# A fused attention and feed-forward kernel: the first VectorE pass over a converted piece of weights is asked for five steps behind GpSimd's clamp in place of two

## The chip, the cores and the metric

The kernel runs on one core of a Trainium2 chip. The metric is the device time of one execution in microseconds (us). Three runs of the kernel before took 936.31, 938.56 and 933.61 us; their median, 936.31 us, is the time before. A further execution was profiled, and all durations below come from it.

The engines are called by their short names: PE (TensorE, the matmuls), DVE (VectorE), ACT (ScalarE), POOL (GpSimd) and SP (SyncE, which here only issues DMAs).

## The reference

The reference is a local and global attention whose output goes through a two-layer feed-forward network with an ELU in between. The weights arrive as float64, and the kernel turns them into pairs of float16 numbers.

```python
# attention: batch 8, heads 8, 512 local and 32 global rows, head_dim 64
s_g = scale * (q_g @ concat(k_g, k_l)^T);  out_g = softmax(s_g) @ concat(v_g, v_l)
s_l = scale * (q_l @ concat(k_g, k_l)^T), local part masked to |i - j| <= 32
out_l = softmax(s_l) @ concat(v_g, v_l)
# feed-forward: x is the attention's output, 4352 rows of 512
h = x @ w_in                       # w_in 512 x 2048, w_out 2048 x 512
g = where(h > 0, h, exp(min(h, 0)) - 1)
return g @ w_out
```

## The kernel before, in words

Two streams of work are written by one loop at the end of `attn_ffn`. The attention goes through its slots in steps, each a stage of scores, softmax, transposes or values. The feed-forward stream (FFN) takes blocks of 256 rows of x: a first product with w_in (L319), the ELU (L329 to L341), and a second product with w_out. The loop tells how many steps of the FFN have to be done by a given step of the attention. In the first 66 steps of the attention, the lead, the FFN does nothing, since no weights are there yet.

The weights come in 16 units of 128 x 1024 numbers: eight pieces (p = 0 to 7) of w_in (m = 0) and eight of w_out (m = 1) in turn. Each goes through these steps (`unit`, from L172):

- `fetch`, L169: SP asks for the raw piece (1 MB) into `raw`, of which there are two buffers. The piece two units later can't be asked for until the last step that reads this one has run.
- s0: ACT takes the absolute value of the upper halves into `cu` (L183), and POOL clamps it (L184). `cu` has three buffers.
- s1a: DVE shifts the clamped number to its place (L188). This is the pinned pass: `keep_in_program_order` holds it at its place in the order in which the code asks for things.
- s1b and s1c: DVE puts in the upper bits (L191) and the lower bits (L195) of the raw piece.
- s1d: ACT takes the absolute value with the largest per partition (L199). It is the last reader of the raw piece.
- s2 and s3, "the spread": the largest over all partitions through a transpose on PE (L136) and a reduction on DVE (L137), then a power of two and its inverse on DVE (L126, L127, L131), and the high float16 part on ACT (L208).
- s4: the low float16 part on DVE (L211).

Steps are put off with `defer(n, fn)`, which runs fn n ticks later; a tick is a step of the attention in the lead, and a step of the FFN stream (about six matmuls) behind it. What a tick sets is when an instruction is asked for. The order in which each engine then runs its instructions is made from that by the tile framework's scheduler when the program is built, which may move an instruction on its engine; only those under `keep_in_program_order` (L188 and the transpose of L136) stay where they were asked for. On the chip each engine runs its instructions strictly in the order so made, and waits at each for what it needs.

The pieces fall into groups: a (piece 0), b (piece 1), c (2 and 3), d (4 to 7). As soon as a group is converted, `tables` makes its scales: the product of the powers on DVE (L227, L228), the largest over the partitions, and the table that `choose` waits for before it gives out a job of that group. The first four blocks of x are computed group by group, and their sums go out to DRAM (`od`) and come back (L451 adds them) for the next group. Once all pieces are converted there is the table "f", and all other blocks are computed in one go with seven products in place of eight (L478).

A job needs x split in float16 parts as well: its largest (L571, and L136/L137 again), a power of two (L126 to L131), the high part on ACT (L565), the low part on DVE (L568), and its scales on POOL (L581 to L585). In the attention, L753 (DVE) and L759 (ACT) are the scores' softmax, L763 and L764 (DVE) and L766 (POOL) its norm, L797 (PE) and L799 (DVE in the lead, ACT behind it) the transposes, L803 (PE) the product with v and L836 (ACT) its copy into x.

Of the kernel before, what the change touches and what calls it, by code (L numbers as in the profile page):

```python
# [60 lines left out]
def attn_ffn(ctx: ExitStack, tc: tile.TileContext, qT, qgT, kT, vT, w_in, w_out, mask, out):  # L61
# [23 lines left out]
    def defer(n, fn):  # L85
        if n == 0:
            return fn()
        later.setdefault(now[0] + n, []).append(fn)
# [10 lines left out]
    lead = [True]  # L99
# [23 lines left out]
    def power(dst, src):  # L123

        dst = dst.bitcast(I32)
        nc.vector.tensor_scalar(dst, src.bitcast(I32), 0x7f800000, None, ALU.bitwise_and)  # L126
        nc.vector.tensor_scalar_max(dst, dst, LOW)  # L127

    def inverse(dst, src):

        nc.vector.tensor_scalar(dst.bitcast(I32), src.bitcast(I32), TOP, -1.0, ALU.subtract, ALU.mult)  # L131

    def all_max(dst, src):

        tp = ps_a.tile([P, 512], F32, name="pa")
        tc.keep_in_program_order(nc.tensor.transpose(tp[:, 0:P], src.to_broadcast([P, P]), ident))  # L136
        nc.vector.tensor_reduce(out=dst, in_=tp[:, 0:P], op=ALU.max, axis=AX.X)  # L137
# [15 lines left out]
    def load_weights():  # L153
        todo = [(group, m, p) for group in "abcd" for p in range(*GROUPS[group]) for m in range(2)]
        raws = [fetch(*todo[0][1:])]
        yield
        for n, (group, m, p) in enumerate(todo):
            if n + 1 < len(todo):
                raws.append(fetch(*todo[n + 1][1:]))
            unit(m, p, raws[n])  # L160
            if (m, p) == (1, GROUPS[group][1] - 1):
                defer(12, lambda group=group: tables(group))
                if p == NP - 1:
                    defer(13, lambda: tables("f"))
            yield

    def fetch(m, p):
        raw = ffn.tile([P, NC, 2 * P, 2] if m == 0 else [P, 2, DM, 2], I32, name="raw")
        nc.sync.dma_start(raw, w1[:, :, 2 * p * P:2 * (p + 1) * P, :] if m == 0 else w2[:, 2 * p:2 * p + 2, :, :])  # L169
        return raw  # L170

    def unit(m, p, raw):  # L172
        f = slice(2 * p * P, 2 * (p + 1) * P)
        shape = [P, NC, 2 * P] if m == 0 else [P, 2, DM]
        parts = [w[:, :, f] for w in win] if m == 0 else [w[:, 2 * p:2 * p + 2, :] for w in wout]
        pw = (pww if m == 0 else pwo)[:, p:p + 1]
        u = ffn.tile(shape, F32, name="cu", bufs=3)
        mx = ffn.tile([P, 4], F32, name="cm", bufs=4)
        high, low = raw[..., 1], raw[..., 0]
        ui = u.bitcast(I32)  # L180

        def s0():
            nc.scalar.activation(u, high.bitcast(F32), AF.Abs)  # L183
            nc.gpsimd.tensor_scalar(u, u, FMAX, FMIN, ALU.min, ALU.max)  # L184

        def s1a():
            tc.keep_in_program_order(
                nc.vector.tensor_scalar(ui, ui, 3, 0x3ffffff8, ALU.logical_shift_left, ALU.bitwise_and))  # L188

        def s1b():  # L190
            nc.vector.scalar_tensor_tensor(out=ui, in0=high, scalar=-0x40000000, in1=ui,  # L191
                                           op0=ALU.bitwise_and, op1=ALU.bitwise_or)

        def s1c():
            nc.vector.scalar_tensor_tensor(out=ui, in0=low, scalar=29, in1=ui,  # L195
                                           op0=ALU.logical_shift_right, op1=ALU.bitwise_or)

        def s1d():
            nc.scalar.activation(low.bitcast(F32), u, AF.Abs, accum_out=mx[:, m:m + 1])  # L199

        def s2():
            if m == 0:
                all_max(mx[:, 1:2], mx[:, 0:1])

        def s3():
            power(pw, mx[:, 1:2])
            inverse(mx[:, 3:4], pw)
            nc.scalar.activation(parts[0], u, AF.Copy, scale=mx[:, 3:4])  # L208

        def s4():  # L210
            nc.vector.scalar_tensor_tensor(out=parts[1].rearrange("p a b -> p (a b)") if m else parts[1],  # L211
                                           in0=u.rearrange("p a b -> p (a b)") if m else u, scalar=mx[:, 3:4],
                                           in1=parts[0].rearrange("p a b -> p (a b)") if m else parts[0],
                                           op0=ALU.mult, op1=ALU.subtract)

        d = 1 if lead[0] else 2
        lag = 7 if m else 16
        for i, fn in ((1, s0), (1 + d, s1a), (1 + 2 * d, s1b), (1 + 3 * d, s1c), (1 + 4 * d, s1d),
                      (1 + lag, s2), (2 + lag, s3), (3 + lag, s4)):
            defer(i, fn)  # L220

    def tables(group):

        r = slice(*GROUPS[group])
        wm = wts.tile([P, 4], F32, name=f"wm_{group}")
        t = wts.tile([P, NP], F32, name=f"t_{group}")
        nc.vector.tensor_mul(t[:, r], pww[:, r], pwo[:, r])  # L227
        nc.vector.tensor_reduce(out=wm[:, 0:1], in_=t[:, r], op=ALU.max, axis=AX.X)  # L228

        def rest():  # L230
            all_max(wm[:, 1:2], wm[:, 0:1])
            nc.vector.reciprocal(wm[:, 2:3], wm[:, 1:2])
            nc.vector.tensor_scalar(t[:, r], pwo[:, r], wm[:, 2:3], 8.0, ALU.mult, ALU.mult)
            nc.vector.tensor_scalar_mul(isc[:, r], pww[:, r], -2.0 ** -28)
            tab[group] = wm[:, 1:2], t

        defer(5, rest)
# [736 lines left out]

    f = ffn_stream()
    units = load_weights()
    done = credit = 0

# [102 lines left out]
```

## Time and profile before

| what | value |
|---|---|
| median of three runs | 936.31 us (933.61 to 938.56) |
| profiled execution | 934.68 us |
| its span (first to last instruction) | 932.9 us |
| mean granted PE clock | 0.979 of full speed |
| the 16 conversion units | the last L188 at 176.4 us |

Three parts follow each other in the span. In the lead, to about 75 us, only the attention and the conversion of the first pieces run. Then the group jobs of the first blocks, the rest of the conversion and the attention run beside each other, to about 230 us. Behind that comes the long stretch of blocks with seven products, in which nothing is converted.

In rows of the timeline the columns are the start in us, the time in us, the engine, the line, the operation, output and input with their tiles, and how many instructions run together; in brackets stands how long the engine was idle before, and what ended the wait. In tables by stretch each engine has its busy time and its number of instructions, then come the granted PE clock, the mean share of the DMA engines and the GB/s.

### The profile page before, as it was taken

The numbers are of one execution on the slowest core, as the hardware profiler recorded it, in microseconds if no ns is written. First come the engines' busy times: TensorE is split into PE (matmuls) and PEld (weight loads), VectorE is DVE, ScalarE is ACT, GpSimd is POOL, SyncE is SP. The second block draws the span as 40 slices with busy tenths as digits, with TensorE's granted clock in tenths as the row PEclk, the third lists the DMA queues.
The fourth block names the chain that finished last, engine by engine and source line by source line (L and its number), as shares of the span: only waits on it lengthen the run. The fifth ranks groups of instructions, "written<-read, shape, count | busy, mean of one in ns | idle before, by whom it ended". The sixth has DMA issues, their size and how long they took to land.

```text
span 932.9 us, 26318 instructions
## 1 busy us (share of the span) xinstructions
PE 888.6 (95%) x10736; PEld 723.2 (78%) x10736; DVE 702.0 (75%) x1945; ACT 637.1 (68%) x1456; POOL 206.2 (22%) x413
## 2 busy tenths in 40 slices
PE   6799889799999999999999999999999999999997
PEld 3466555467676788888888888888888888888886
DVE  4869889899957768777786768786868677766566
ACT  5669888676566567675776767676766676656564
POOL 4556461441321022011122112112111121200000
PEclk7789999899999999999999999999999999999999
DMA  7957867432442134012521234103312111000000
GB/s 259 351 202 263 305 232 239 138 103 92 159 162 67 60 126 167 30 48 72 186 87 49 69 126 149 49 24 133 141 48 63 54 47 47 1 24 24 1 24 23
DMA packets 39472, 103.60 MB, mean 111 GB/s; under 512 B 5944, under 2 KB 6584, under 8 KB 39352
## 3 DMA queue, kind: packets, MB, share of 16 engines
q1 hardware_dynamic: 39064, 101.66, 31.6%
q8 instruction: 84, 1.38, 0.6%
q14 instruction: 36, 0.29, 0.1%
q10 hardware_dynamic: 288, 0.26, 0.1%
HBM read 86.70 MB, written 15.20 MB: 109 GB/s over the span
## 4 chain that ended last, share of the span: by engine, by line
PE 50%; DVE 22%; ACT 18%; DMA 5%; issue 3%; POOL 2%; SPq 0%; DVEq 0%; ACTq 0%; POOLq 0%
PE pa L319 19%; PE acc L478 9%; PE h L478 7%; ACT p L759 5%; DVE gl L341 4%; ACT gh L357 3%; DVE gx L338 3%; PE acc L443 3%; PE pa L803 3%; PE h L319 2%; DMA raw<-w_out 2%; PE pa L797 2%; DMA od<-o 2%; ACT g L329 2%; ACT g L331 2%
## 5 line engine op out<-in xcount | busy, mean ns | idle before, releaser
L319 PEld LDWEIGHTS <-winh 128*128 128x128 f16 x2160 | 209.7, 98 | 36.3 <-issue 6.6
L319 PE MATMUL pa<-xh,winh 128*128 128x256 f16 x824 | 224.9, 273 | 0.8 <-DVE xglob L873 0.8
L319 PE MATMUL pa<-xl,winh 128*128 128x256 f16 x824 | 224.7, 273 | 0.0
L319 PE MATMUL pa<-xh,winl 128*128 128x256 f16 x824 | 224.7, 273 | 0.0
L357 ACT ACTIVATE gh<-gx,xs 128x896 f16<-128x896 f32 x103 | 107.5, 1044 | 132.8 <-DVE gx L354 132.8
L766 POOL TENSOR_SCALAR p<-p,sm 128x128 f32<-128x128 f32 x256 | 117.5, 477 | 328.8 <-DVE sm L764 297.7
L341 DVE SCALAR_TENSOR_TENSOR gl<-gx,xs,gh 128x896 f16<-128x896 f32 x103 | 122.5, 1189 | 75.4 <-ACT gh L357 75.4
L478 PEld LDWEIGHTS <-gh 128*128 128x128 f16 x1456 | 140.1, 98 | 22.6 <-issue 7.0
L319 PEld LDWEIGHTS <-winl 128*128 128x128 f16 x1080 | 106.0, 98 | 16.5 <-issue 3.7
L759 ACT ACTIVATE p<-p,m 128x128 f32<-128x128 f32 x256 | 99.3, 390 | 25.8 <-DVE m L753 25.7
L478 PE MATMUL acc<-wouth,gh 128*128 128x256 f16 x312 | 85.3, 273 | 0.0
L478 PE MATMUL acc<-wouth,gl 128*128 128x256 f16 x312 | 85.1, 273 | 0.0
L331 ACT ACTIVATE g<-g 128x512 f32<-128x512 f32 x135 | 85.0, 630 | 0.1
L478 PE MATMUL acc<-woutl,gh 128*128 128x256 f16 x312 | 85.1, 273 | 0.0
L478 PEld LDWEIGHTS <-gl 128*128 128x128 f16 x728 | 71.2, 98 | 9.3 <-DVE gl L341 1.0
L329 ACT ACTIVATE g<-pa,xs 128x512 f32<-128x512 f32 x103 | 70.2, 681 | 9.7 <-PE pa L319 9.1
L478 PE MATMUL h<-raw,gh 128*128 128x256 f16 x416 | 74.3, 273 | 0.0
L319 PE MATMUL h<-xl,winh 128*128 128x256 f16 x256 | 70.7, 277 | 3.3 <-DVE xl L568 3.3
L319 PE MATMUL h<-xh,winh 128*128 128x256 f16 x256 | 70.6, 277 | 3.2 <-ACT hs L330 2.1
L319 PE MATMUL h<-xh,winl 128*128 128x256 f16 x256 | 70.7, 277 | 0.0
L803 PEld LDWEIGHTS pa<-pt,v 128*64 128x64 f32 x1728 | 53.3, 139 | 8.0 <-issue 6.3
L338 DVE SCALAR_TENSOR_TENSOR gx<-g,p 128x512 f32<-128x512 f32 x52 | 37.7, 725 | 28.3 <-ACT g L331 26.8
(219 smaller groups left out, 1878.0 us busy)
## 6 DMA issues: line engine op xcount, KB each, us to landing
v<-vT SPq DMA_DIRECT2D x64, 512.0 KB, 4.6
k<-kT SPq DMA_DIRECT2D x32, 640.0 KB, 5.2
q<-qT SPq DMA_DIRECT2D x32, 256.0 KB, 5.9
raw<-w_in SPq DMA_DIRECT2D x8, 1024.0 KB, 5.7
raw<-w_out SPq DMA_DIRECT2D x8, 1024.0 KB, 7.0
out<-o SPq DMA_DIRECT2D x32, 256.0 KB, 2.3
od<-o SPq DMA_DIRECT2D x24, 256.0 KB, 3.3
o<-od SPq DMA_DIRECT2D x24, 256.0 KB, 2.8
```

Source lines behind the costliest of these rows:

```text
L319: nc.tensor.matmul(h[:, j, :], wt[:, c, f], xt[:, c, :], start=k == 0, stop=k == 11)
L329: nc.scalar.activation(g, hf, AF.Relu, scale=sc[:, p:p + 1])
L331: nc.scalar.activation(g, g, AF.Exp, scale=-1.0)
L338: nc.vector.scalar_tensor_tensor(out=out, in0=ins[0], scalar=-1.0, in1=ins[1], op0=ALU.add, op1=ALU.max)
L341: nc.vector.scalar_tensor_tensor(out=dst, in0=src, scalar=sg, in1=hi, op0=ALU.mult, op1=ALU.subtract)
L357: nc.scalar.activation(gh, gx, AF.Copy, scale=sg)
L443: nc.tensor.matmul(acc[t], gt[:, s], wt[:, f, :], start=p == first and j == 0 and k == 0, stop=p == last and j == 1 and k == 2)
L478: nc.tensor.matmul(cols, gt, w, start=p == 0 and k == 0, stop=last and k == len(todo) - 1, skip_group_check=True)
L759: nc.scalar.activation(ps[i], ps[i], AF.Exp, bias=m[:, i:i + 1], scale=-1.0, accum_out=s[:, 0, i:i + 1])
L766: nc.gpsimd.tensor_scalar(ps[i], ps[i], s[:, 1, i:i + 1], 1.0, ALU.mult, ALU.mult)
L797: nc.tensor.transpose(tp[:, h * P:(h + 1) * P], st["p", g, t][:, h, :], ident)
L803: nc.tensor.matmul(o[:, to:to + n], st["v", g, t][:, 4 * h + w, :], st["pt", g, t][:, h, at:at + n], start=start, stop=True, skip_group_ch ...
```

## The change

All offsets are counted in ticks from the moment at which a unit is taken up; s0, with the clamp, stands at 1 in both kernels.

| step | lead before | lead now | behind the lead before | behind it now |
|---|---|---|---|---|
| s1a (L188) | 2 | 4 | 3 | 6 |
| s1b (L191) | 3 | 5 | 5 | 8 |
| s1c (L195) | 4 | 6 | 7 | 10 |
| s1d (L199) | 5 | 7 | 9 | 12 |
| s2 of w_out's units | 8 | 9 | 8 | 12 |
| s2 of w_in's units | 17 | 17 | 17 | 21 |
| tables of a group | 12 | 12 | 12 | 16 |
| tables "f" | 13 | 17 | 13 | 17 |

```diff
             if (m, p) == (1, GROUPS[group][1] - 1):
-                defer(12, lambda group=group: tables(group))
+                defer(12 if lead[0] else 16, lambda group=group: tables(group))
                 if p == NP - 1:
-                    defer(13, lambda: tables("f"))
+                    defer(17, lambda: tables("f"))
...
-        d = 1 if lead[0] else 2
-        lag = 7 if m else 16
-        for i, fn in ((1, s0), (1 + d, s1a), (1 + 2 * d, s1b), (1 + 3 * d, s1c), (1 + 4 * d, s1d),
+        d, wait = (1, 3) if lead[0] else (2, 5)
+        lag = (11 if m else 20) if not lead[0] else (8 if m else 16)
+        for i, fn in ((1, s0), (1 + wait, s1a), (1 + wait + d, s1b), (1 + wait + 2 * d, s1c), (1 + wait + 3 * d, s1d),
                       (1 + lag, s2), (2 + lag, s3), (3 + lag, s4)):
             defer(i, fn)
```

Both programs have the same instructions, 1947 on DVE and 14340 on PE among them; only their order on the engines differs, and that only from the third unit to the end of the conversion. Three places follow.

The first is DVE in the lead, around the pinned pass of the fourth unit. L799 is a copy of transposed softmax rows, L763 and L764 belong to a norm, `cm` and `pww` to a spread. Before:

```order
L799 COPY pt<-pa 128x2x4x64
L763 TENSOR_SCALAR sm<-sm 128x4
L137 TENSOR_REDUCE cm<-pa 128x1
L764 RECIPROCAL sm<-sm 128x4
L188 TENSOR_SCALAR cu<-cu 128x1024
L126 TENSOR_SCALAR pww<-cm 128x1
```

And now:

```order
L188 TENSOR_SCALAR cu<-cu 128x1024
L763 TENSOR_SCALAR sm<-sm 128x4
L799 COPY pt<-pa 128x2x4x64
L764 RECIPROCAL sm<-sm 128x4
L137 TENSOR_REDUCE cm<-pa 128x1
L191 SCALAR_TENSOR_TENSOR cu<-raw,cu 128x1024
L126 TENSOR_SCALAR pww<-cm 128x1
```

The pinned pass now stands ahead of the copy and of the norm's two small steps, and L191 ahead of the spread's L126.

The second is PE at the same place in the lead. L803 are the products with v of one slot, L797 the four transposes of another slot's softmax rows (p_83). Before:

```order
L741 MATMUL pa<-k,q 32x128 x16
L803 MATMUL h<-pt,v 64x32 x2
L797 MATMUL pa<-ident,p_83 128x128 x4
L803 MATMUL h<-pt,v 64x64 x4
L803 MATMUL h<-pt,v 64x32 x4
L803 MATMUL h<-pt,v 64x64 x4
L803 MATMUL h<-pt,v 64x32 x2
L728 MATMUL pa<-ident,pg_82 128x128 x2
```

And now:

```order
L803 MATMUL h<-pt,v 64x32 x2
L803 MATMUL h<-pt,v 64x64 x4
L803 MATMUL h<-pt,v 64x32 x4
L803 MATMUL h<-pt,v 64x64 x4
L803 MATMUL h<-pt,v 64x32 x2
L797 MATMUL pa<-ident,p_83 128x128 x4
L728 MATMUL pa<-ident,pg_82 128x128 x2
```

The four transposes have moved from within the products with v to behind them.

The third is DVE at the end of the conversion, around the split of a block of x (`xm`, `xl`) for that block's first job; the last two units are in work. Before, from the last but one unit's L191 to the last unit's L188; L568 follows eleven rows on, behind five scores' reductions (L753):

```order
L191 SCALAR_TENSOR_TENSOR cu<-raw,cu 128x1024
L714 TENSOR_REDUCE sg<-sg 128x1
L127 TENSOR_SCALAR xm<-xm 128x1
L195 SCALAR_TENSOR_TENSOR cu<-raw,cu 128x1024
L715 TENSOR_SCALAR sg<-sg 128x1
L131 TENSOR_SCALAR xm<-xm 128x1
L753 ISA p_85,m<-pa,msk 128x128
L753 ISA m 128x1
L716 RECIPROCAL sg<-sg 128x1
L188 TENSOR_SCALAR cu<-cu 128x1024
```

And now, the last unit's L188 standing seventeen rows behind the end of this piece:

```order
L127 TENSOR_SCALAR xm<-xm 128x1
L131 TENSOR_SCALAR xm<-xm 128x1
L188 TENSOR_SCALAR cu<-cu 128x1024
L714 TENSOR_REDUCE sg<-sg 128x1
L191 SCALAR_TENSOR_TENSOR cu<-raw,cu 128x1024
L211 SCALAR_TENSOR_TENSOR woutl<-cu,cm,wouth 128x1024
L715 TENSOR_SCALAR sg<-sg 128x1
L568 SCALAR_TENSOR_TENSOR xl<-xr,xm,xh 128x1024
L716 RECIPROCAL sg<-sg 128x1
L195 SCALAR_TENSOR_TENSOR cu<-raw,cu 128x1024
```

The small steps of the split (L127, L131) now stand ahead of the last but one unit's passes, and L568 ahead of the last unit's L188 and of all scores' reductions.

## The prediction

> **What bounds the kernel now.** I read the page first, then the busy times by stretch, then the waits of the pinned pass, and last the timeline of DVE, ACT, POOL and PE at the places where the order changes. The page says that PE is the bound over the whole:
>
> ```profile
> span 932.9 us, 26318 instructions
> PE 888.6 (95%) x10736; PEld 723.2 (78%) x10736; DVE 702.0 (75%) x1945; ACT 637.1 (68%) x1456; POOL 206.2 (22%) x413
> ```
>
> So time can come only from what PE spends idle (932.9 − 888.6 = 44.3 us) or at a lower clock. The table by stretch says where that is (the columns: stretch, length, busy time of each engine, granted PE clock, DMA share, GB/s):
>
> ```profile
> 0.00:77.00 77.00, 61.37 (x936) 38.59 (x937) 54.86 (x240) 49.44 (x170) 39.90 (x80) 0.82 0.75 272
> 77.00:112.00 35.00, 32.36 (x430) 22.12 (x427) 29.96 (x91) 31.26 (x74) 17.64 (x29) 0.95 0.82 277
> 112.00:135.00 23.00, 19.17 (x182) 14.28 (x167) 19.98 (x41) 21.62 (x39) 12.88 (x18) 1.00 0.78 263
> 135.00:173.00 38.00, 33.91 (x319) 20.07 (x323) 35.43 (x72) 30.12 (x56) 9.93 (x12) 1.00 0.74 231
> 173.00:186.00 13.00, 8.16 (x70) 5.42 (x55) 9.26 (x33) 7.96 (x24) 8.07 (x18) 0.74 0.19 65
> 186.00:932.00 746.00, 733.68 (x8838) 622.69 (x8835) 552.50 (x1472) 496.69 (x1098) 117.77 (x259) 1.00 0.22 77
> ```
>
> Behind 186 us PE is busy 733.68 of 746: whatever the change wins or loses earlier is carried through to the end. Ahead of it PE is idle for 15.63 us in the lead, 2.64, 3.83 and 4.09 in the three stretches from 77 to 173, and 4.84 in the 13 us at the conversion's end. The whole effect must come from there. The waits of the pinned pass are the obvious target:
>
> ```profile
> DVE cu L188 <- POOL cu L184: 6.8, 6, 2.1
> ```
>
> Six of the 16 passes waited for their clamp, 6.8 us in sum, 2.1 the longest. That is a ceiling only for what DVE gets back; PE gets it back only where PE or ACT waited for DVE behind it.
>
> **The change part by part.** The instructions are the same, so nothing is added or removed, and each term is a move. I took the places where the order differs and put the durations of before into the order of now.
>
> *Lead, 41 to 55 us.* Here are the rows of DVE, POOL, PE and ACT:
>
> ```profile
> 41.86 0.69 DVE L799 COPY pt<-pa 128x512 f32<-128x512 f32 x1
> ...
> 42.82 0.66 DVE L188 TENSOR_SCALAR cu<-cu 128x1024 int32<-128x1024 int32 x1
> ...
> 43.67 1.22 DVE L191 SCALAR_TENSOR_TENSOR cu<-raw,cu 128x1024 int32<-128x1024 int32 x1
> ```
>
> ```profile
> 41.07 0.37 POOL L766 TENSOR_SCALAR p<-p,sm 128x128 f32<-128x128 f32 x1
> 41.52 1.04 POOL L184 TENSOR_SCALAR cu<-cu 128x1024 f32<-128x1024 f32 x1
> 43.07 5.17 POOL L766 TENSOR_SCALAR p<-p,sm 128x128 f32<-128x128 f32 x8 [0.51 <-ACT p L759]
> ```
>
> ```profile
> 46.56 0.82 PE L797 MATMUL pa<-ident,p 128*128 128x128 f32 x2 [0.90 <-POOL p L766]
> ...
> 47.32 1.71 PE L803 MATMUL h<-pt,v 128*64 128x64 f32 x28
> ```
>
> ```profile
> 49.07 0.37 ACT L836 COPY xr<-h 128x256 f32<-128x256 f32 x1 [4.66 <-PE h L803]
> ...
> 50.97 1.13 ACT L199 ACTIVATE raw<-cu 128x1024 f32<-128x1024 f32 x1
> ```
>
> Before, the products L803 began, then stood behind four transposes that wait for POOL's norms, and ran on only at 47.32; ACT waited 4.66 us for them. Now the products go first. They need the copy L799. That copy now stands behind the pinned pass, which waits for the clamp's end at 41.52 + 1.04 = 42.56: the pass ends at 43.2, L763 at 43.4, the copy at 44.1. The 32 products then take about 2 us and end near 46.1, where they ended at 49.03, and ACT's L836 comes at 46.1 in place of 49.07. Behind it ACT's L199 would come up to 3.3 us earlier (50.97 less about 47.6). Against that, the norm's L764 comes behind the copy at 44.1 to 44.3, so POOL's eight norms begin at 44.3 in place of 43.07, 1.2 us later, and the transposes behind them end as much later. The bounds are −3.3 (all of ACT's gain reaches PE) and +1.2 (only the norms' delay does). I take −1.5, between them and nearer to the gain, since 4.66 us is the longer wait and the rest of the lead has 15.63 us of PE idle time to take up delays.
>
> *Group jobs, 77 to 135 us.* No order gets simpler here; the raw pieces come later. The rows are:
>
> ```profile
> 106.79 1.14 ACT L199 ACTIVATE raw<-cu 128x1024 f32<-128x1024 f32 x1
> ...
> 119.65 1.18 ACT L183 ACTIVATE cu<-raw 128x1024 f32<-128x1024 f32 x1
> ...
> 125.66 0.67 ACT L330 ACTIVATE hs<-h,xs 128x512 f32<-128x512 f32 x1
> ```
>
> ```profile
> 108.03 0.38 SPq L169 DMA_DIRECT2D raw<-w_out  x1
> ```
>
> ```profile
> raw<-w_out SPq DMA_DIRECT2D x8, 1024.0 KB, 7.0
> ```
>
> ```profile
> 120.92 1.20 POOL L184 TENSOR_SCALAR cu<-cu 128x1024 f32<-128x1024 f32 x1 [5.79 <-ACT cu L183]
> ```
>
> ```profile
> 126.38 0.27 PE L319 MATMUL h<-xh,winh 128*128 128x256 f16 x1 [1.24 <-ACT hs L330]
> ```
>
> The eighth unit's L199 (106.79) now stands on ACT behind a block's L565 and the ninth unit's L183, so at 113.6 or later, 7 us later. SP's request for the tenth unit's piece, which waits for it, goes from 108.03 to about 115, and with 7.0 us of landing ACT's L183 goes from 119.65 to about 122, the clamp's end from 122.12 to about 124.4. On POOL the scales of a job of group c now stand behind that clamp. So the evictions L329 and L330 wait for the scales, and L330 goes from 125.66 to about 127. PE waited for it already at 126.38, for 1.24 us; six matmuls of a second product that now stand ahead fill about as much. I take +0.5. Bounds: −1, if those six matmuls fill the old wait of 1.24 and nothing is late; +3.7, if the 2.4 us of L183 and the 1.3 us of L330 both reach PE, one behind the other.
>
> *135 to 173 us.* Two of the pinned pass's waits lie here, 2.6 us of DVE, and ACT has waits of its own, for landing pieces:
>
> ```profile
> ACT cu L183 <- DMA raw<-w_out: 2.5, 3, 2.1
> ```
>
> Three waits, 2.5 us, the longest 2.1. The pass's waits go; ACT's grow, since the last reader of a piece comes three ticks later and the piece is asked for as much later. A tick is about six matmuls, and the row from 112 to 135 gives 19.17 / 182 = 0.105 us for one, so three ticks are 1.9 us, called 2 from here; where DVE's shorter waits give half of it back, a piece comes 1 us later. One is set against the other: 0, with bounds −2 (DVE's 2.6 us less what PE is not waiting for) and +2.5 (ACT's waits double).
>
> *The conversion's end, 173 to 186 us.* This is the place with the most idle PE time, and the largest term:
>
> ```profile
> 169.33 1.29 DVE L211 SCALAR_TENSOR_TENSOR woutl<-cu,cm,wouth 128x1024 f16<-128x1024 f32 x1
> ...
> 173.97 0.14 DVE L131 TENSOR_SCALAR xm<-xm 128x1 int32<-128x1 int32 x1
> ...
> 176.44 0.69 DVE L188 TENSOR_SCALAR cu<-cu 128x1024 int32<-128x1024 int32 x1 [2.05 <-POOL cu L184]
> ...
> 178.10 1.61 DVE L568 SCALAR_TENSOR_TENSOR xl<-xr,xm,xh 128x1024 f16<-128x1024 f32 x1
> ```
>
> ```profile
> 172.78 1.20 ACT L183 ACTIVATE cu<-raw 128x1024 f32<-128x1024 f32 x1 [0.18 <-DMA raw<-w_out]
> ...
> 174.12 1.13 ACT L199 ACTIVATE raw<-cu 128x1024 f32<-128x1024 f32 x1
> ...
> 175.22 1.16 ACT L565 ACTIVATE xh<-xr,xm 128x1024 f16<-128x1024 f32 x1
> ...
> 184.71 0.69 ACT L329 ACTIVATE g<-h,xs 128x512 f32<-128x512 f32 x1 [3.49 <-POOL p L766]
> ```
>
> ```profile
> 176.42 0.38 PE L319 MATMUL h<-xh,winh 128*128 128x256 f16 x2 [0.71 <-ACT xh L565]
> ...
> 179.76 0.37 PE L319 MATMUL h<-xl,winh 128*128 128x256 f16 x1 [2.96 <-DVE xl L568]
> ```
>
> ```profile
> 177.50:184.20 6.70, 4.44 (x22) 3.05 (x22) 6.70 (x24) 2.91 (x14) 2.32 (x6) 0.50 0.00 0
> ```
>
> Before: the pinned pass waited 2.05 us for its clamp, with five scores' reductions and the split's L568 queued behind it; PE waited 2.96 us for that, and then ran at a clock of 0.50 for 6.7 us. Now L568 stands ahead of the pass. Its chain is shorter too: the split's L131 no longer waits behind L191 and L195 and comes near 171.0 in place of 173.97, L565 near 173.1 in ACT's free time in place of 175.22, and L568 near 174.4 to 176.0 in place of 178.10 to 179.71. That is 3.7 us for PE's first product. What is late next is ACT: L183 waits for its piece (which landed at 172.78 by the row's wait, and lands near 173.8 with the 1 us from above), behind it come L199 and eight exponentials, and I put L329 at 181.9, where it stood at 184.71: −2.8. If all 3.7 come through and the clock holds, the gain is larger: at a clock of 0.50 matmuls take twice as long, so 4.44 us busy would be about 2.2. The far end is thus 3.7 + 2.2, with some of the 0.71 ahead: −6.5. The other end is 0, if the piece lands so late that ACT's queue stands where it stood. I take −3.0, next to the −2.8 of ACT's queue. The cover of the pinned pass, now behind all this, are the reductions of two slots; without it DVE would wait the 2.05 us again, but with nobody behind it that PE needs.
>
> Tables "f" come four ticks later and the last transpose with them. PE has matmuls of group d's jobs to do until then, as many more as it takes, so I cost that at nothing; in the 746 us behind 186 PE was idle 12.3 us, and if that cover failed it would be some 1.5 us more.
>
> The sum is −1.5 + 0.5 + 0 − 3.0 = −4.0 us: 934.68 becomes 930.7. The profiled execution lies 1.63 us below the median of the three runs; against 936.31 the sum is 932.3. A measurement of this kernel can tell about 0.5%, 4.7 us, from no change: faster begins below 931.6, slower above 941.0.
>
> Two rules of the Trainium skill bear on it. The row of 0.50 from 177.5 to 184.2 follows a PE wait of 2.96 us and a stretch of thin work. The Trainium skill, "TensorE: Matmul & The Clock Gate", section on the HAM clock gate, says that the array drops to half rate after an idle window of about 3.4 us and comes back after a busy one; by that rule a shorter wait could save the whole slow stretch, and the trace agrees in so far as the slow stretch has 0.50 and follows a wait. The other row is POOL's: eight norms took 5.17 us, 0.65 each, while DVE ran L191 and L195, against 0.37 for one ahead of them. The Trainium skill, "SBUF — State Buffer", section on who interferes with whom, says that a VectorE instruction with two inputs in SBUF and a GpSimd instruction that reads SBUF shut each other out for a whole instruction. It speaks against the change in the lead: norms that begin 1.2 us later meet the same two passes, so by it that term would be +1.2, and the sum −1.3.
>
> **The rivals.** *The clock too.* If PE's first product comes 3.7 us earlier and the wait of 2.96 us shrinks, the half clock from 177.5 may not be granted at all, and the last term is −6.5 in place of −3.0; with the lead's −1.5 and nothing for the others that is −8.0, 928.3. For it: behind 186 us the clock is 1.00, and the stretch of 0.50 stands right behind that wait. Against: PE does only 8.16 us in that stretch of 13, so there are other holes in which the clock may go.
>
> *Waits only move.* PE finds as much to wait for as before, since each chain that is shorter ends in ACT's queue, which is busy 30.12 and 21.62 us of 38 and 23. Then it is 936.3. For it: DVE is at 35.43 of 38 us between 135 and 173, and its 6.8 us of waits are idle time of an engine which PE mostly didn't wait for. That the change doesn't do what it says is no case here, since the order of the engines shows it.
>
> *Raw pieces become late.* s1d is the last reader of a piece, and there are two buffers. With s1d three ticks (2 us) later, a piece that lands 7.0 us after its request comes behind the moment at which ACT reaches L183, and ACT stands in front of evictions that PE needs. It decides when a request comes less than 7.0 us ahead of L183, as it did for three units (2.5 us of waits). If each of the three pays the 2 us, and the gains don't come through, the sum is +6: 942.3, slower. For it: the tenth unit, where my own count puts the request 7 us later. Against: the same row counts only three such waits, so most pieces have landed when ACT gets there.
>
> **How the numbers follow.** The forecast has 0.55: two of its four terms rest on an order that shows a wait gone, with PE behind it. The clock has 0.12, the waits that only move 0.18, the late pieces 0.15. The forecast's own range, by bounds that don't all fall on one side, is 929.3 to 934.8, and nearly half of it lies below 931.6 (0.25 of 0.55). Faster by over 0.5% is thus 0.25 + 0.12 = 0.37, slower the most of the late pieces, 0.13, and the same 0.50. The range that leaves out no more than 2 in 10 goes from 926.0 (the clock, and the lead's −3.3) to 940.0, which leaves out the late pieces at their price.
>
> **What would show it.** In the profile of the changed kernel the pinned pass's waits for the clamp should be near nothing outside the lead. PE's wait for L568 at 179.76 should come near 176 and be shorter, ACT's L329 that followed it near 182, and PE busy over 8.16 us in the 13 us there. In the lead, ACT's wait of 4.66 us for L803 should shrink to under 2, and the norms begin 1 us later. Between 105 and 125 us the request of SP should come near 115. I am wrong if the stretch from 77 to 173 us gets longer by over 2.5 us, if ACT's waits for landing pieces pass 5 us in sum, or if PE's start of the long stretch is no earlier than before.

## The result and the profile after

The changed kernel is slower. Eighteen runs of it took 942.52 us in the median (938.57 to 947.09), eighteen runs of the kernel before 935.67 (933.61 to 939.42): a ratio of 1.0064, with a 95% interval of 1.0051 to 1.0077. I had forecast 932.3 against 936.31, a ratio of 0.996. The profiled execution took 939.22 us, 4.5 more than that of before; with 942.52 for the median it is one of the faster ones. Two single runs, one of h2_last_reader below (1292.22 us) and one of the kernel before (1139.78 us), had a granted clock of 0.65 and 0.74, far under that of all others, and no ratio contains them. The page of the kernel after:

```profile
span 937.4 us, 26326 instructions
PE 887.5 (95%) x10736; PEld 721.7 (77%) x10736; DVE 701.4 (75%) x1945; ACT 638.0 (68%) x1456; POOL 215.8 (23%) x413
```

PE has the same work as before (887.5 us against 888.6) in a longer span: it is idle for longer. The table by stretch, with the same columns as before:

```profile
0.00:77.00 77.00, 59.68 (x916) 36.31 (x917) 53.49 (x235) 48.42 (x163) 39.81 (x77) 0.82 0.73 265
77.00:112.00 35.00, 31.63 (x405) 22.22 (x405) 27.62 (x77) 30.17 (x73) 13.07 (x20) 0.95 0.80 270
112.00:135.00 23.00, 20.31 (x196) 14.18 (x195) 18.78 (x53) 19.43 (x41) 14.77 (x23) 1.00 0.72 257
135.00:173.00 38.00, 31.58 (x265) 19.12 (x265) 33.85 (x66) 31.28 (x52) 12.59 (x17) 1.00 0.66 215
173.00:186.00 13.00, 10.41 (x126) 7.28 (x125) 11.61 (x39) 8.88 (x24) 9.21 (x11) 1.00 0.53 164
```

In the last row the reader sees what I had forecast: PE is busy for 10.41 us of the 13 where it was 8.16, and the granted clock is 1.00 where it was 0.74. But PE was busy for 1.7 us less in the lead, and for 2.3 less from 135 to 173. Nor does the loss end at 186 us. Here are the 24 us behind it, first before, then after:

```profile
186.00:210.00 24.00, 22.70 (x160) 15.35 (x158) 21.62 (x45) 19.05 (x32) 10.94 (x16) 1.00 0.31 100
```

```profile
186.00:210.00 24.00, 18.10 (x126) 11.90 (x124) 20.34 (x47) 19.13 (x39) 13.71 (x22) 1.00 0.24 89
```

PE does 4.6 us less there. The waits of PE between 173 and 212 us say on what (who waited for whom: us in total, times, longest). Before:

```profile
PE h L319 <- DVE xl L568: 3.0, 1, 3.0
...
PE acc L443 <- DVE o L451: 0.9, 1, 0.9
```

After:

```profile
PE acc L443 <- DVE o L451: 2.1, 1, 2.1
PE h L319 <- ACT p L330: 1.9, 1, 1.9
PE h L319 <- DVE xl L568: 1.8, 1, 1.8
PE acc L443 <- DVE pwo L127: 1.5, 1, 1.5
```

One long wait became shorter (the split's L568, 3.0 to 1.8), and three others came or grew behind it by 4.6 us in sum. They stand where the last pieces are converted, and the conversion ends later. ACT takes up the last unit's piece at 182.28 us, 9.5 us later than before (172.78), after 3.25 us of waiting for it:

```profile
182.28 1.15 ACT L183 ACTIVATE cu<-raw 128x1024 f32<-128x1024 f32 x1 [3.25 <-DMA raw<-w_out]
```

From 77 to 232 us ACT's waits for landing pieces have grown from 2.5 to 7.0 us:

```profile
ACT cu L183 <- DMA raw<-w_out: 4.4, 2, 3.2
...
ACT cu L183 <- DMA raw<-w_in: 2.6, 1, 2.6
```

The request for the sixth unit's piece, the first of those whose passes all lie behind the lead, is later as well. SP in the lead, before and then after:

```profile
59.90 8.81 SPq L681 DMA_DIRECT2D v<-vT  x3
68.81 0.39 SPq L169 DMA_DIRECT2D raw<-w_out  x1
```

```profile
59.20 11.89 SPq L681 DMA_DIRECT2D v<-vT  x3
71.19 0.39 SPq L169 DMA_DIRECT2D raw<-w_out  x1
```

SP issues in order, and the request stands behind three loads of v that wait for a free buffer, so for the attention. The attention is late, and the request with it. It showed 68.81 before and 71.19 now, and the first L319 went from 71.88 to 74.28:

```profile
74.28 0.27 PE L319 MATMUL h<-xh,winh 128*128 128x256 f16 x1 [0.84 <-DVE xglob L841]
```

One profile alone can't settle differences of 2 us: an experiment below whose lead has the old order (e2_behind) still has its first L319 at 73.55.

### The profile page after: what moved, and what is told of

It is laid out like the page before. It is cut to its first block, busy times and chain, and to the rows that moved or that the text cites. A ratio compares the mean times of both kernels' runs of the same rounds, so it can differ in the third digit from the quotient of the medians.

```text
span 937.4 us, 26326 instructions
## 1 busy us (share of the span) xinstructions
PE 887.5 (95%) x10736; PEld 721.7 (77%) x10736; DVE 701.4 (75%) x1945; ACT 638.0 (68%) x1456; POOL 215.8 (23%) x413
## 4 chain that ended last, share of the span: by engine, by line
PE 49%; DVE 23%; ACT 16%; issue 4%; DMA 4%; POOL 3%; SPq 0%; DVEq 0%; ACTq 0%; POOLq 0%
PE pa L319 19%; PE acc L478 9%; PE h L478 7%; ACT p L759 5%; DVE gl L341 4%; ACT gh L357 3%; PE acc L443 3%; DVE gx L338 3%; PE pa L803 3%; PE pa L797 2%; PE h L319 2%; POOL p L766 2%; DMA raw<-w_out 2%; PE pa L693 2%; PE pa L741 2%
## 5 line engine op out<-in xcount | busy, mean ns | idle before, releaser
L319 PEld LDWEIGHTS <-winh 128*128 128x128 f16 x2160 | 209.2, 98 | 35.7 <-issue 6.8
L319 PE MATMUL pa<-xh,winh 128*128 128x256 f16 x824 | 224.8, 273 | 0.9 <-DVE xglob L873 0.9
L319 PE MATMUL pa<-xh,winl 128*128 128x256 f16 x824 | 224.6, 273 | 0.0
L319 PE MATMUL pa<-xl,winh 128*128 128x256 f16 x824 | 224.6, 273 | 0.0
L766 POOL TENSOR_SCALAR p<-p,sm 128x128 f32<-128x128 f32 x256 | 119.7, 486 | 340.2 <-DVE sm L764 298.0
L319 PEld LDWEIGHTS <-winl 128*128 128x128 f16 x1080 | 105.7, 98 | 14.6 <-issue 1.9
L478 PEld LDWEIGHTS <-gl 128*128 128x128 f16 x728 | 71.2, 98 | 9.2 <-DVE gl L341 1.0
L329 ACT ACTIVATE g<-pa,xs 128x512 f32<-128x512 f32 x103 | 70.2, 682 | 9.8 <-PE pa L319 9.2
L319 PE MATMUL h<-xh,winh 128*128 128x256 f16 x256 | 69.7, 273 | 3.5 <-ACT p L330 1.9
L319 PE MATMUL h<-xl,winh 128*128 128x256 f16 x256 | 69.7, 273 | 1.8 <-DVE xl L568 1.8
L319 PE MATMUL h<-xh,winl 128*128 128x256 f16 x256 | 69.7, 273 | 0.0
L803 PEld LDWEIGHTS pa<-pt,v 128*64 128x64 f32 x1728 | 53.3, 138 | 10.3 <-issue 7.5
L338 DVE SCALAR_TENSOR_TENSOR gx<-g,p 128x512 f32<-128x512 f32 x52 | 37.8, 728 | 28.3 <-ACT g L331 27.0
```

The lines of the kernel that those rows point to most:

```text
L319: nc.tensor.matmul(h[:, j, :], wt[:, c, f], xt[:, c, :], start=k == 0, stop=k == 11)
L329: nc.scalar.activation(g, hf, AF.Relu, scale=sc[:, p:p + 1])
L338: nc.vector.scalar_tensor_tensor(out=out, in0=ins[0], scalar=-1.0, in1=ins[1], op0=ALU.add, op1=ALU.max)
L478: nc.tensor.matmul(cols, gt, w, start=p == 0 and k == 0, stop=last and k == len(todo) - 1, skip_group_check=True)
L766: nc.gpsimd.tensor_scalar(ps[i], ps[i], s[:, 1, i:i + 1], 1.0, ALU.mult, ALU.mult)
L803: nc.tensor.matmul(o[:, to:to + n], st["v", g, t][:, 4 * h + w, :], st["pt", g, t][:, h, at:at + n], start=start, stop=True, skip_group_ch ...
```

## The experiments

Sixteen kernels ran, four at a time on one chip beside runs of the kernel before, 7 to 12 times each. "Ratio" is time against that kernel, with its 95% interval. The other columns come from the profiled execution of each: SP's request for the sixth unit's piece, the start of the first L319, of ACT's L183 and of L208 of the last unit, and the execution's time (us).

| kernel | ratio | request | first L319 | last L183 | last L208 | time |
|---|---|---|---|---|---|---|
| before | 1 | 68.8 | 71.88 | 172.78 | 190.81 | 934.68 |
| after | 1.0064 (1.0051 to 1.0077) | 71.2 | 74.28 | 182.28 | 194.95 | 939.22 |
| e1_lead | 0.9998 (0.9977 to 1.0019) | 71.0 | 74.15 | 175.06 | 193.42 | 937.77 |
| e2_behind | 1.0014 (0.9996 to 1.0032) | 70.5 | 73.55 | 180.11 | 193.13 | 938.51 |
| e3_passes | 0.9998 (0.9980 to 1.0015) | 69.3 | 72.40 | 181.63 | 196.96 | 938.79 |
| e4_tables | 0.9998 (0.9981 to 1.0015) | 68.6 | 71.69 | 177.47 | 190.85 | 936.31 |
| g1_after_again | 1.0051 (1.0031 to 1.0071) | 71.6 | 75.91 | 185.28 | 198.67 | 943.89 |
| g2_passes_lead | 1.0023 (1.0006 to 1.0041) | 72.0 | 75.09 | 180.97 | 195.97 | 938.36 |
| g3_tables_lead | 1.0019 (0.9996 to 1.0042) | 72.2 | 75.63 | 178.07 | 191.45 | 937.03 |
| g4_early_release | 1.0008 (0.9987 to 1.0028) | 72.2 | 76.49 | 179.47 | 195.41 | 940.63 |
| h1_before_early | 0.9994 (0.9973 to 1.0015) | 70.1 | 73.16 | 173.23 | 189.80 | 934.27 |
| h2_last_reader | 1.0036 (1.0014 to 1.0059) | 72.6 | 75.67 | 183.00 | 196.89 | 942.42 |
| h3_behind_early | 0.9991 (0.9972 to 1.0009) | 69.1 | 72.22 | 174.11 | 190.74 | 935.89 |
| h4_lead_passes | 0.9976 (0.9954 to 0.9998) | 66.1 | 71.43 | 173.76 | 191.47 | 935.82 |
| k1_old_lead_spread | 0.9991 (0.9973 to 1.0009) | 66.2 | 71.59 | 175.88 | 190.53 | 934.64 |
| k5_held_raw | 1.0020 (1.0006 to 1.0035) | 72.1 | 76.39 | 179.68 | 194.01 | 939.51 |
| k3_old_spread_early | 0.9950 (0.9931 to 0.9968) | 66.2 | 71.58 | 169.25 | 185.16 | 930.20 |
| k4_lead_passes_early | 0.9941 (0.9922 to 0.9961) | 66.4 | 71.74 | 168.19 | 185.15 | 929.56 |

### The change in halves

e1_lead, against the kernel before; in this and the next the offsets of the passes are written with `wait` as in the change:

```diff
-        d = 1 if lead[0] else 2
-        lag = 7 if m else 16
+        d, wait = (1, 3) if lead[0] else (2, 2)
+        lag = (8 if m else 16) if lead[0] else (7 if m else 16)
```

> Only the lead part of the change: three steps behind the clamp in place of one in the lead, w_out's spread one step later there, all else as before. The changed kernel is 0.64% (6.0 us) slower in the median. In its trace the first feed-forward matmuls of the lead start 2.4 us later (74.28 against 71.88 us). Theory A, the lead is a part of it: this kernel is 2 us slower than before (ratio 1.002), and its first L319 starts near 74. Theory B, everything lies behind the lead and the 2 us are taken up there: ratio 1.000. My recorded forecast would have it at -1.5 us (0.998).

Measured: 0.9998, and the first L319 at 74.15. The 2 us showed in the lead and not in the time, so theory B (everything behind the lead) is nearer.

e2_behind, against the kernel before:

```diff
-        d = 1 if lead[0] else 2
-        lag = 7 if m else 16
+        d, wait = (1, 1) if lead[0] else (2, 5)
+        lag = (7 if m else 16) if lead[0] else (11 if m else 20)
...
-                defer(12, lambda group=group: tables(group))
+                defer(12 if lead[0] else 16, lambda group=group: tables(group))
...
-                    defer(13, lambda: tables("f"))
+                    defer(17, lambda: tables("f"))
```

> Only the part of the change behind the lead: five steps behind the clamp, spreads and tables four steps later; the lead as before. Theory A (parts add): +4 us, ratio 1.004, and together with the lead part alone the 6.0 us of the change. Theory B: the whole +6 us, 1.0064. My recorded forecast would have it at -2.5 us (0.997).

Measured: 1.0014. Neither theory holds: the halves don't add up to 1.0064.

e3_passes and e4_tables take the part behind the lead apart, against e2_behind:

```diff
-        lag = (7 if m else 16) if lead[0] else (11 if m else 20)
+        lag = (7 if m else 16) if lead[0] else (10 if m else 16)
...
-                defer(12 if lead[0] else 16, lambda group=group: tables(group))
+                defer(12 if lead[0] else 14, lambda group=group: tables(group))
...
-                    defer(17, lambda: tables("f"))
+                    defer(15, lambda: tables("f"))
```

> Behind the lead only the passes L188 to L199 come three ticks later; w_in's spread stays at its old tick, w_out's spread and the tables come only as much later as the later L199 forces (w_out's spread behind L199, group tables 14 in place of 12, f 15 in place of 13). If the late last reader of the raw piece and the late passes are what costs (theory C, my recorded rival of late pieces), it keeps most of the loss: +4 us, ratio 1.004. If late tables and spreads cost (theory D): +2 us or less, 1.002.

```diff
-        d, wait = (1, 1) if lead[0] else (2, 5)
+        d, wait = (1, 1) if lead[0] else (2, 2)
```

> Behind the lead only the spreads and the tables come four ticks later, as in the change; the passes stay two ticks behind the clamp. Theory C (late passes and pieces cost): no change, ratio 1.000. Theory D (late tables and spreads cost): +4 us, 1.004.

Measured: 0.9998 for both. Late passes (theory C) and late tables (theory D) each cost nothing that was measured by themselves. From 77 to 232 us ACT waits 6.0 us for landing pieces in e3_passes, and the time doesn't change; those waits are not a price in themselves:

```profile
ACT cu L183 <- DMA raw<-w_out: 5.1, 3, 2.7
ACT cu L183 <- DMA raw<-w_in: 0.9, 1, 0.9
```

### Whether the halves act on each other

g1_after_again is the change itself; g2_passes_lead and g3_tables_lead each put one thing of it back:

```diff
-        lag = (11 if m else 20) if not lead[0] else (8 if m else 16)
+        lag = (10 if m else 16) if not lead[0] else (8 if m else 16)
...
-                defer(12 if lead[0] else 16, lambda group=group: tables(group))
+                defer(12 if lead[0] else 14, lambda group=group: tables(group))
...
-                    defer(17, lambda: tables("f"))
+                    defer(15, lambda: tables("f"))
```

```diff
-        d, wait = (1, 3) if lead[0] else (2, 5)
+        d, wait = (1, 3) if lead[0] else (2, 2)
```

> The changed kernel as it is, a second time, beside the kernels that change one half of it. The lead part alone measured 0.9998 and the part behind the lead alone 1.0014, which do not add up to 1.0064. Theory E (the halves act on each other: a late lead meets late pieces): again 1.0064, some 6 us. Theory F (they do add, and the two sets of runs differ by something else): 1.002 or less, as the part behind the lead alone.

> The changed kernel with w_in's spread behind the lead at its old tick (17 in place of 21), w_out's one tick earlier (11), group tables at 14 and f at 15; lead and passes as in the change. Under theory E, if the passes are what the lead acts on: 1.006. If the late tables are: about 1.000, as the passes alone measured (0.9998). Theory F: 1.000 either way.

> The changed kernel with the passes behind the lead back at two ticks behind the clamp; lead, spreads and tables as in the change. Under theory E, if late tables are what the lead acts on: 1.006; if the late passes and pieces are: about 1.000. Theory F: 1.000 either way.

Measured: 1.0051, 1.0023 and 1.0019. The loss is there again, so theory F falls. Lead, passes and tables each alone give 1.000, two of them about 1.002 (1.0014, 1.0023, 1.0019), all three 1.005 to 1.006. That is the pattern which delays on one path that share a slack (time by which a step can be late before anything waits for it) would give, though the intervals of those with two overlap with their neighbours' on both sides.

### The raw pieces

g4_early_release lets L199 write elsewhere; its written value isn't used, only its accumulated one, so nothing else of the computation changes:

```diff
-            nc.scalar.activation(low.bitcast(F32), u, AF.Abs, accum_out=mx[:, m:m + 1])
+            nc.scalar.activation(parts[0], u, AF.Abs, accum_out=mx[:, m:m + 1])
```

> The changed kernel, but L199 writes its unused result over the float16 part that L208 fills later, and no longer into the raw piece, so that the piece is free behind L195 and the next piece can be asked for some 2 us earlier. Theory C (late pieces cost, my recorded rival): most of the loss goes, 1.002 or less, and the requests of L169 come earlier in the trace. If late pieces are not the cause: as slow as the changed kernel run beside it, 1.006.

Measured: 1.0008 where the changed kernel beside it had 1.0051. From there came theory G. h1_before_early and h3_behind_early are the same edit in the kernel before and in e2_behind:

> The kernel before, with L199's unused result written over the float16 part that L208 fills later, so that the raw piece is free behind L195. Theory G (three delays share one slack: the lead's 3 us, the late pieces' 4 us, the late tables' 2 us; each alone fits into the slack, and only what goes beyond it shows): pieces that were not late here have nothing to give, ratio 1.000. Theory C in its plain form (pieces that land late cost in any case; ACT waits 2.5 us for them here): 2 us faster, 0.998.

> The part of the change behind the lead, with the lead as before, and the raw pieces freed early as in the run that did so with the whole change (1.0008). Theory G: neither the lead nor the pieces are late, only the tables, and the slack takes these: 1.000. If a shorter wait of the pinned pass is worth anything by itself, as my recorded forecast had it, it shows here: 0.997.

Measured: 0.9994 and 0.9991, nearer to theory G, though the first interval contains theory C's 0.998 as well. h2_last_reader and k5_held_raw are to hold the piece and leave the passes early. The first is against the change, the second against g3_tables_lead:

```diff
+        back = wait if lead[0] else 2
-        for i, fn in ((1, s0), (1 + wait, s1a), (1 + wait + d, s1b), (1 + wait + 2 * d, s1c), (1 + wait + 3 * d, s1d),
+        for i, fn in ((1, s0), (1 + back, s1a), (1 + back + d, s1b), (1 + back + 2 * d, s1c), (1 + wait + 3 * d, s1d),
```

```diff
-                      (1 + lag, s2), (2 + lag, s3), (3 + lag, s4)):
+                      *(() if lead[0] else ((12, lambda: nc.vector.tensor_copy(mx[:, 2:3], high[:, 0, 0:1].bitcast(F32))),)), (1 + lag, s2), (2 + lag, s3), (3 + lag, s4)):
```

> The changed kernel with the three DVE passes behind the lead back at two ticks behind the clamp (3, 5, 7), and only L199, the last reader of the raw piece, left at its late tick (12); lead, spreads and tables as in the change. The same kernel with L199 at its old tick measured 1.0019. Theory G with late pieces as its second delay: the loss comes back, 1.005 or more, and ACT waits for landing pieces for 6 us or more between 77 and 232 us. If it is the late DVE passes themselves: 1.002.

> The kernel with the late lead and the late tables, but the old passes (it measured 1.0019), and with one tiny DVE copy more per unit behind the lead, which reads one column of the raw piece at the tick at which the change has L199, so that only the piece is held longer. Theory G with late pieces as its third delay: 1.005, the requests of L169 late as in the changed kernel, and ACT's waits for landing pieces 6 us or more between 77 and 232 us. If the late DVE passes themselves are the delay and not the pieces: 1.002.

Measured: 1.0036 and 1.0020. Neither settles it. In h2_last_reader ACT waited 5.9 us for landing pieces and the last L183 came 4.9 us later than in g3_tables_lead, as theory G had it, but the time lies between the two forecasts and its interval contains both. In k5_held_raw the edit didn't do what it was meant to: the copy needs nothing but the landed piece, and the scheduler put it ahead of L199 in seven of the eleven units, by 2.2 to 11.6 us; in the other four it starts 0.4 to 2.3 us behind L199's start. So the piece was hardly held, ACT waited 2.0 us for landing pieces and not 6, and the time is that of the kernel without the copy (1.0019). That holding a piece costs is not shown, and that it costs nothing isn't either.

### The lead

h4_lead_passes is e1_lead with w_out's spread at its old step:

```diff
-        lag = (8 if m else 16) if lead[0] else (7 if m else 16)
+        lag = 7 if m else 16
```

> The kernel before, with the passes in the lead three steps behind the clamp and w_out's spread there at its old step. In four profiles with the new lead the first L319 starts at 74.2 to 76.5 us, in four with the old lead at 71.7 to 73.6. If the later passes make the lead late: it starts near 75 here too. If the spread does: near 72. In the time, as the whole lead part alone: 1.000.

Measured: 0.9976, and the first L319 at 71.43: of the lead's two moves it is the spread's step that makes it late, and only together with the late passes, since with the old passes that step leaves the order of all engines as it was. k1_old_lead_spread takes this one number back in the change:

```diff
-        lag = (11 if m else 20) if not lead[0] else (8 if m else 16)
+        lag = (11 if m else 20) if not lead[0] else (7 if m else 16)
```

> The changed kernel, but with w_out's spread in the lead back at its old step (8 in place of 9); all else as in the change. With the late passes in the lead but the old spread step the first L319 started at 71.4 us, with both late at 74.2 to 76.5. Theory G (three delays, of which the slack takes about one): the lead's delay goes, what is left are late pieces and late tables, as in the part behind the lead alone: 1.0015, and the first L319 near 72. If the lead's delay is not one of the causes: 1.0055, as the changed kernel.

Measured: 0.9991. Taking back one step of one number in the lead takes away the whole loss, more than theory G gave it. It is not the only thing that does much: taking back the late tables (g2_passes_lead) or the late passes (g3_tables_lead), or freeing the pieces early (g4_early_release), took away over half of it by the medians. Its SP and PE in the lead:

```profile
56.72 9.41 SPq L681 DMA_DIRECT2D v<-vT  x3
66.22 0.39 SPq L169 DMA_DIRECT2D raw<-w_out  x1
```

```profile
71.59 0.27 PE L319 MATMUL h<-xh,winh 128*128 128x256 f16 x1
```

The request goes out at 66.22 where it went out at 71.19 and 71.63 in the two profiles of the change, and the last L183 comes at 175.88 where it came at 182.28 and 185.28. k3_old_spread_early is this kernel with the pieces freed early, k4_lead_passes_early is h4_lead_passes with it (the edit is that of g4_early_release):

> The changed kernel with w_out's spread in the lead at its old step and with the raw pieces freed early (L199's unused result written over the float16 part that is filled later). Theory G: only the late tables are left, and the slack takes them: 0.999. If the pinned pass five steps behind the clamp gains anything once its three costs are taken away, it shows here: 0.997.

> The kernel before with the late passes in the lead alone (it measured 0.9976 in ten runs) and with the raw pieces freed early (0.9994 alone): the two that came out lowest, together. If the 0.9976 is a gain: 0.997. If it is a draw of the spread of runs: 0.999 to 1.000.

Measured: 0.9950 and 0.9941, both clear of 1 and faster than both kernels of this case. The second has everything behind the lead but the release as it was, so this gain is not one of the later passes there. The last L183 of k3_old_spread_early:

```profile
169.25 1.15 ACT L183 ACTIVATE cu<-raw 128x1024 f32<-128x1024 f32 x1
```

It comes 6.6 us earlier than in k1_old_lead_spread, and doesn't wait. From h4_lead_passes to k4_lead_passes_early it is 5.6 us, and from e2_behind to h3_behind_early 6.0. In the kernel before the same edit brought nothing forward there (173.23 against 172.78), and nothing in the time.

## Why the prediction was wrong

In the 18 profiles the time goes with the end of the conversion. Between the start of the last unit's L208 and the time of the same execution the correlation is 0.96, with 0.95 us per us; for the last L183 it is 0.94, with 0.73. That alone names no cause: both contain whatever was late earlier, and e3_passes, whose last L208 is the second latest (196.96), has a ratio of 0.9998. I had judged the change by the waits next to each place whose order it alters, and not by what a delay there does to the end of the chain of 16 units.

*Lead, −1.5.* At the place itself the working held in this profile: I put L836 at 46.1, L199 at about 47.6 and POOL's norms at 44.3. ACT and POOL of the kernel after:

```profile
46.17 0.37 ACT L836 COPY xr<-h 128x256 f32<-128x256 f32 x1 [1.60 <-PE h L803]
...
47.48 1.16 ACT L199 ACTIVATE raw<-cu 128x1024 f32<-128x1024 f32 x1
```

```profile
44.63 4.88 POOL L766 TENSOR_SCALAR p<-p,sm 128x128 f32<-128x128 f32 x8 [1.65 <-ACT pt L729]
```

That it fits to some 0.3 us is luck in part: in the second profile of the change (g1_after_again) L836 starts at 47.35, after a wait of 2.98 us where I had named under 2, and L199 at 48.67. The norms ended 1.3 us later than before (49.51 against 48.24), which didn't decide: where nothing else was moved (h4_lead_passes) the norms end at 49.20, and the lead's passes came out as a gain, 0.9976 or 2.2 us, if barely (the interval reaches 0.9998).

**The step that failed is that I ended the lead's term at 55 us and gave w_out's spread, one step later, no term at all.** From 56 to 74 us that step changes the order. Here are the first block's L565 and L568, in the kernel after and then in k1_old_lead_spread:

```profile
63.75 1.13 ACT L565 ACTIVATE xh<-xr,xm 128x1024 f16<-128x1024 f32 x1
```

```profile
66.19 1.27 DVE L568 SCALAR_TENSOR_TENSOR xl<-xr,xm,xh 128x1024 f16<-128x1024 f32 x1
```

```profile
59.52 1.15 ACT L565 ACTIVATE xh<-xr,xm 128x1024 f16<-128x1024 f32 x1 [0.88 <-DVE xm L131]
```

```profile
60.70 1.30 DVE L568 SCALAR_TENSOR_TENSOR xl<-xr,xm,xh 128x1024 f16<-128x1024 f32 x1
```

The first L319 is 2.7 us and the request of SP 5 us later than there. Against the kernel before the lead's term is +2.4 us at the first L319 and not −1.5; in the mean of the eight profiles with the change's lead it starts at 75.5, of the six with the old one at 72.5. Taken back, the step removes the whole loss of the change, 1.0064 and 1.0051 to 0.9991, some 6 us. Behind the lead these two kernels have the same order on all engines, and the delay is there from the lead on: the kernel after is behind k1_old_lead_spread by 5.3 us at the fifth unit's L199 and by 4.4 to 5.6 at all later ones.

With the old passes behind the lead the same step costs less: from h4_lead_passes to e1_lead the ratio goes only from 0.9976 to 0.9998, with intervals that overlap. There the delay is 5.3 us at the fifth unit's L199 and 5.2 at the twelfth, but only 1.2 to 2.0 at the last three. In between h4_lead_passes, the earlier one, runs into a wait, ACT for the fourteenth unit's piece and PE behind it:

```profile
153.53 1.12 ACT L183 ACTIVATE cu<-raw 128x1024 f32<-128x1024 f32 x1 [2.83 <-DMA raw<-w_out]
```

```profile
156.99 0.47 PE L136 MATMUL pa<-ident,cm 128*128 128x128 f32 x1 [3.40 <-ACT raw L199]
```

In e1_lead the same two waits are 0.28 and 0.90 us. So in this pair there was slack that took up most of the delay, and in the other pair there was none. The sizes are rough: two profiles of the change itself differ by up to 4.2 us at these places.

*Group jobs, +0.5.* The lateness was right in kind and a little short: I put the tenth unit's request at 115 and its L183 at 122; they came at 117.75 and 123.55.

*135 to 173, 0.* This failed too. I set ACT's growing waits against DVE's shrinking ones and had a piece come 1 us later; the last came 9.5 us later, and PE's busy time in the stretch fell by 2.3 us. I had counted the passes' delay once, for one unit. It comes again in each unit: from L183 to L199 it is 10.4 us in the mean of the ninth to fourteenth unit after, 9.2 before. But neither is a price by itself: k1_old_lead_spread, which loses nothing, has 10.4 us there too, and PE is busy even less in that stretch (31.36 us against 31.58).

*The end, −3.0.* At the place itself the mechanism held: L568 ahead of the pinned pass, PE's wait 1.77 in place of 2.96, no half clock. Here it is in PE's timeline:

```profile
180.97 0.27 PE L319 MATMUL h<-xl,winh 128*128 128x256 f16 x1 [1.77 <-DVE xl L568]
```

But all of it happened later, so L329 came at 187.54 and not at 181.9. Behind it PE waited 1.9, 1.5 and 2.1 us, where I had named a cover for the late tables and costed them at nothing, with a bound of 1.5 us. That these waits are the tables' is not shown, nor are they the loss: k1_old_lead_spread waits 2.0 us for L451, 2.0 for L127 and 1.9 for L568 in the same stretch and loses nothing. And no kernel shows the term as a gain: e2_behind, which has all of it with the old lead, measured 1.0014. The pass's waits for the clamp, which I had near nothing outside the lead, went from 5.1 us in four there to 2.5 in two.

*The rivals.* The clock did stay up in that stretch, as the first rival had it, but PE did 4.6 us less in the next 24 us, and the second profile of the change has a half clock of 3.4 us from 197.9. I had also misread where the half clock of before comes from. It began at 177.43, 0.6 us after the wait of 2.96 us had begun (176.80), so it can't follow it; ahead of it stand 3.4 us in which PE was busy for 0.90:

```profile
174.02:177.43 3.41, 0.90 (x4) 0.34 (x4) 1.36 (x9) 2.74 (x6) 3.15 (x9) 1.00 0.26 77
```

The late pieces had the sign and, by chance, the size (942.3). Their mechanism, ACT's waits times three, is refuted as a price by e3_passes and h1_before_early, which wait 6.0 and 6.4 us and lose nothing; that those waits passed 5 us, which I had named as a sign of being wrong, came true (7.0). One sum in the prediction is off: the lower end of the range, by its own terms (−6.5 and −3.3 from 936.31), is 926.5 and not 926.0.

*What stays open.* That the spread's step costs 2 us with the old passes behind the lead and 6 with the late ones fits one path with a shared slack. The slack was seen in one pair of profiles, and no run takes it alone away. Why the early release helps is open too. It went with 0.2 to 0.4% less time in the four kernels whose lead or whose passes were late (in two pairs the intervals overlap), but it alters the order on several engines as well, and the two kernels that were to hold a piece longer don't settle it. Whether the gain is the earlier landing or the new order isn't settled.

## What to carry to other kernels

Where a change puts steps off in a chain that feeds everything behind it, follow the chain to its end and sum the delay per turn; a wait that goes beside it tells little. Give every number that the change touches its own term, the smallest too: here taking back one step of one offset took away the whole loss, and with the input buffer freed one step earlier as well the kernel gained 0.5%. When parts measure nothing alone, measure them in pairs before calling them harmless. And where an instruction is added to hold a buffer, look in the trace whether it runs where it was meant to.

## What the runs showed of the hardware

The time of a run goes with its granted clock: over the 18 runs of the changed kernel the clock lay between 0.970 and 0.982, with a correlation of −0.82 and 0.6 us per 0.001. Two profiles of this kernel show how: the second is 1.6 us behind the first at the fourth L338 (98.84 against 97.25) and 4.1 at the fifth (129.45 against 125.35), and in between the clock is at 0.50 for 6.8 us in the second (105.8 to 112.6) and for 3.4 in the first (104.7 to 108.1). So two single executions of one program can differ by some 4 us.

POOL's norms slow down beside a DVE instruction with two inputs in SBUF. POOL and DVE of the kernel after, and POOL of k1_old_lead_spread without such a neighbour:

```profile
66.18 2.49 POOL L766 TENSOR_SCALAR p<-p,sm 128x128 f32<-128x128 f32 x4
```

```profile
66.19 1.27 DVE L568 SCALAR_TENSOR_TENSOR xl<-xr,xm,xh 128x1024 f16<-128x1024 f32 x1
```

```profile
64.15 1.41 POOL L766 TENSOR_SCALAR p<-p,sm 128x128 f32<-128x128 f32 x4
```

Four norms took 2.49 us and 1.41, and PE waited 1.23 us for them in the lead of the kernel after. In k1_old_lead_spread the L581 that starts at 60.80, beside the L568 shown above, took 1.34 us, and the next L581 0.26. The Trainium skill, "SBUF — State Buffer", section on who interferes with whom, says that a DVE instruction with two inputs in SBUF and a POOL instruction that reads SBUF shut each other out for a whole instruction; the 1.1 us more in both cases agree with that, L568 taking 1.27 to 1.30.
